# One tile's attention scores put beside the preceding tile's state and output, and the state products in two halves of the array

## The chip, the cores and the metric

The kernel runs on one core of a Trainium2 chip. TensorE (PE in the profile) multiplies matrices into PSUM, VectorE (DVE), ScalarE (ACT) and GpSimd (POOL) work on tiles, and SyncE (SP) issues most transfers. The metric is the device time of one execution in microseconds.

## The reference

A linear attention with decay, then two feed-forward parts. With B = 4, H = 8, S = 768, D = 48:

```python
for t in range(S):
    cur = np.einsum('bhd,bhe->bhde', u[None] * kt, vt)
    y[:, :, t] = np.einsum('bhd,bhde->bhe', rt, state + cur)
    state = wt[:, :, :, None] * state + np.einsum('bhd,bhe->bhde', kt, vt)
...
x = y as (3072, 384)
h = x @ w_in                                   # 384 x 2048
x = (h * clip(h + 3, 0, 6) / 6) @ w_out        # 2048 x 384
h = x @ w_in2                                  # 384 x 1024
solu = h * softmax(h); ln = layernorm(solu) * g_ln
out = ln @ w_out2                              # 1024 x 384
```

## The kernel before

**Tiles.** The sequence is cut into 6 groups of 128 steps; with 4 batches that is 24 tiles (`NTILE`), tile i being group i // 4 of batch i % 4. A tile's attention has five stages, `stw`, `st0`, `st1`, `st2`, `st3`.

`stw` clamps the decays w. `st0` brings w and r into the layout with channels on the partitions (for tiles up to 9 by transposes on TensorE, from tile 10 on, `LATE`, by VectorE's transposes in `flip`, L427) and makes running products of the decays by scans (L484, L490): q, from the end of the tile, and e, r times the inverse. `st1` brings k (kt), makes the decayed state sp and its remainder sr on GpSimd (L508, L512), q = kt times q (L518), and z = r k u. `st2` transposes q back to tokens (ktp, L532; copied to ktok by ScalarE, L534) and makes the scores pa of eight heads, the even ones on the lower, the odd ones on the upper half of the partitions (L543); GpSimd makes the masks am from the diagonal d (L550) and VectorE copies the scores into them (L554). `st3` makes the state products kv = ktok x v, two heads in one full-array product of which the diagonal blocks are used (L563), the output yt from the decayed state (L578) and from the scores (L585), four column strips of 32 at a time, the new state s_st = kv + sp (L604), and the two rounded halves of the output, xh and xl (L616, L617).

**Dense work.** The first feed-forward part goes in 96 slots (`NSLOT`), 16 for each group of four tiles: in slot n `ffn_in(n)` makes h by nine products of 512 columns (L635), ScalarE and VectorE make t, gh and gl from it (L639 to L643), and two slots later `ffn_out` uses them in nine products for y (L655). So a slot has eighteen dense products. In slots 0 to 12 the weights are still decoded (`w1_a`, `w1_b`), largely on VectorE.

**Order.** Attention stages of tiles 4 to 23 are put between `ffn_in(n)` and `ffn_out(n - 2)` by the table `sched`: tile i has `stw`, `st0`, `st1` and `st2` in the slots 4(i - 4) - 3, - 2, - 1 and 0 and `st3` in 4(i - 4) + 2. So in four slots one has the scores of a tile (`st2`), and the one two later has its output (`st3`) and the next tile's `st0`. The program order is a priority: a planner walks it with costs of its own and lets a ready instruction go ahead of one that isn't. Buffers in rotation set what can be ready: `ps_a` has three PSUM buffers that kt, wt, rt, ktp, pa, kv and yt share, `ps_h` two for h, and am has two, both of one tile. sp has one.

Of the kernel before, what the change touches and what calls it, by code (L numbers as in the profile page):

```python
# [8 lines left out]
F32 = mybir.dt.float32  # L9
# [4 lines left out]
ALU = mybir.AluOpType  # L14
# [4 lines left out]
P = 128  # L19
# [248 lines left out]
def fast_path(  # L268
# [14 lines left out]
    nc = tc.nc  # L283
    B, H, S, D = r.shape
# [5 lines left out]
    HP = H // 2  # L290
    DP = 112
# [4 lines left out]
    NTILE = NG * B  # L296
    NSLOT = NG * M1
    LAG = 2
    LATE = 10

    const = ctx.enter_context(tc.tile_pool(name="const", bufs=1, side="left"))
    dram = ctx.enter_context(tc.tile_pool(name="dram", bufs=1, space=DRAM))
# [20 lines left out]
    ps_h = left.enter_context(tc.tile_pool(name="ps_h", bufs=2, space=PSUM, side="left"))  # L323
# [6 lines left out]
        out=causal.bitcast(F32), in_=ones, pattern=[[1, P]], compare_op=ALU.is_gt, fill=0.0, base=0,  # L330
# [5 lines left out]
    atp = right.enter_context(tc.tile_pool(name="atp", bufs=2, side="right"))  # L336
# [24 lines left out]
    def w1_a(m):  # L361
        wst[m].append(dec_a(nc, dec, wst[m][0]))

    def w1_b(m):
        split(nc, dec_b(nc, *wst.pop(m)), w1_h[:, m, :], w1_l[:, m, :], nc.vector)


    s_st = []
# [5 lines left out]
    at = {}  # L374
    x_t = {}

    def load_in(i):
        g, b = divmod(i, B)
        t0 = g * C
        a = {}  # L380
        for nm, src, spare in (("w", w, "gh"), ("r", r, "gl"), ("k", k, "t")):
            if i == 2:
                t = ffp.tile([P, H, 64], F32, tag=spare, name=nm, bufs=2 if spare == "t" else 3)
            else:
                t = inp.tile([P, H, 64], F32, tag=nm, name=nm)
            nc.gpsimd.memset(t[:, :, D:64], 1.0)
            nc.sync.dma_start(out=t[:, :, 0:D], in_=src[b, :, t0:t0 + C, :].rearrange("h t d -> t h d"))
            a[nm] = t
        at[i] = a
# [34 lines left out]
    def flip(nm):  # L424

        t = ps_tile(nm + "t")
        nc.vector.transpose(  # L427
            out=t.rearrange("p h (b j) -> p h j b", j=4),
            in_=late[nm].rearrange("p h (j d) -> p h j d", d=D)[:, :, :, 0:32],
        )  # L430
        return t

    def ps_tile(nm):
        return ps_a.tile([P, 4, P], F32, tag="pa", name=nm)

    def trans(dst, src):
        s2 = src.rearrange("p h d -> p (h d)")
        for hp in range(HP):
            nc.tensor.transpose(out=dst[0:DP, hp, :], in_=s2[:, hp * P:hp * P + DP], identity=ident)

    def stw(i):
        a = at[i]
        if i >= LATE:
            x = late["w"][:, :, 0:4 * D - 16]
# [25 lines left out]
    def st0(i):  # L470
        a = at[i]
        g = i // B
        if i < LATE:
            wt = ps_tile("wt")
# [22 lines left out]
    def st1(i):  # L497
        a = at[i]
        g, b = divmod(i, B)
        q = a["q"]  # L500
        if i < LATE:
            kt = ps_tile("kt")
            trans(kt, a["k"])
        else:
            kt = flip("k")
        if g > 0:
            sp = atp.tile([P, HP, 2 * D], F32, tag="sp", name="sp", bufs=1)
            nc.gpsimd.tensor_tensor(  # L508
                out=sp[0:DP], in0=s_st[b][0:DP], in1=q[0:DP, :, 0:1].to_broadcast([DP, HP, 2 * D]), op=ALU.mult
            )  # L510
            sr = atp.tile([P, HP, 32], F32, tag="sr", name="sr", bufs=1)
            nc.gpsimd.tensor_tensor(  # L512
                out=sr[0:DP].rearrange("p h (j d) -> p h j d", j=2),
                in0=s_st[b][0:DP].rearrange("p h (j d) -> p h j d", j=2)[:, :, :, 32:D],
                in1=q[0:DP, :, 0:1].unsqueeze(3).to_broadcast([DP, HP, 2, D - 32]), op=ALU.mult,
            )
            a["sp"], a["sr"] = sp, sr
        nc.vector.tensor_tensor(out=q[0:DP, :, 1:C + 1], in0=kt[0:DP], in1=q[0:DP, :, 1:C + 1], op=ALU.mult)  # L518
        z = a["r"][:, :, 0:D]
        nc.gpsimd.tensor_tensor(out=z, in0=z, in1=a["k"][:, :, 0:D], op=ALU.mult)  # L520
        nc.gpsimd.tensor_tensor(out=z, in0=z, in1=u_bc, op=ALU.mult)
        a["z"] = z

    def st2(i):
        a = at[i]
# [30 lines left out]
    def st3(i):  # L556
        a = at[i]
        g, b = divmod(i, B)
        if g < NG - 1:
            vv = a["v"].rearrange("p h d -> p (h d)")  # L560
            kv = ps_tile("kv")
            for hp in range(HP):
                nc.tensor.matmul(  # L563
                    out=kv[0:DP, hp, 0:2 * D], lhsT=a["ktok"][:, hp, :], rhs=vv[:, hp * 2 * D:(hp + 1) * 2 * D],
                    start=True, stop=True,
                )
        y = ps_tile("yt")

        def inter(c, first):
            for q in range(4):  # L570
                if c < 2:
                    h = 4 * c + q
                    hp, f = h // 2, D * (h % 2)
                    lhs = a["sp"][0:DP, hp, f:f + 32]
                else:
                    hp = q
                    lhs = a["sr"][0:DP, q, :]
                nc.tensor.matmul(  # L578
                    out=y[32 * q:32 * q + 32, c, :], lhsT=lhs, rhs=a["e"][0:DP, hp, :], start=first, stop=not first,
                    skip_group_check=True,  # L580
                )

        def intra(c, heads, lo, n, first, last):
            for q, h in enumerate(heads):
                nc.tensor.matmul(  # L585
                    out=y[32 * q:32 * q + n, c, :], lhsT=a["v"][:, h, lo:lo + n], rhs=a["am"][h % 2][:, h // 2, :],
                    start=first, stop=last, skip_group_check=True,
                )

        for c in range(2):  # L590
            if g > 0:
                inter(c, True)
            intra(c, range(4 * c, 4 * c + 4), 0, 32, g == 0, True)
        intra(2, range(1, H, 2), 16, 32, True, False)
        intra(2, range(0, H, 2), 32, 16, True, g == 0)
        if g > 0:
            inter(2, False)
        if g < NG - 1:
            for j in range(2):
                o, f = 64 * j, D * j  # L600
                dst = s_st[b][o:o + D, :, f:f + D]
                src = kv[o:o + D, :, f:f + D]
                if g > 0:
                    nc.vector.tensor_tensor(out=dst, in0=src, in1=a["sp"][o:o + D, :, f:f + D], op=ALU.add)  # L604
                else:
                    nc.scalar.activation(out=dst, in_=src, func=ACTF.Copy)
        at.pop(i)
        if b == 0:
            x_t[g] = (
                xp.tile([P, KD, GT], F32R, tag="xh", name="xh"),  # L610
                xp.tile([P, KD, GT], F32R, tag="xl", name="xl"),
            )
        xh, xl = x_t[g]
        sl = slice(b * C, (b + 1) * C)
        xf = y[:, 0:KD, :]
        nc.scalar.activation(out=xh[:, :, sl], in_=xf, func=ACTF.Copy, accum_out=chk[:, 3 * i + 2:3 * i + 3])  # L616
        nc.vector.tensor_tensor(out=xl[:, :, sl], in0=xf, in1=xh[:, :, sl].bitcast(F32), op=ALU.subtract)  # L617
# [110 lines left out]
    def load_to(n):  # L728
        while nxt[0] < min(n, LATE):
            load_in(nxt[0])  # L730
            load_v(nxt[0])
            nxt[0] += 1
# [15 lines left out]
    NS = len(stages)  # L748
    for tick in range(starts[-1] + NS):
        for i in range(B):  # L750
            s = tick - starts[i]
# [13 lines left out]
    sched = {}  # L765
    for i in range(B, NTILE):
        for s in range(NS):
            sched.setdefault(4 * (i - B) + (s - 3 if s < NS - 1 else 2), []).append((i, s))
    for n in sorted(q for q in sched if q < 0):
        for i, s in sched[n]:  # L770
            stages[s](i)
# [2 lines left out]
    for n in range(NSLOT + LAG):  # L774
        if n < NSLOT:
            ffn_in(n)
        for i, s in sorted(sched.get(n, [])):
            stages[s](i)
            if s == 3:
                load_to(i + 3)  # L780
            if s == 2 and LATE <= i + 1 < NTILE:
                load_late(i + 1)
        if n >= LAG:
            ffn_out(n - LAG)
        if n + LD < M1:
            w1_b(n + LD)
        if n + LD + 1 < M1:
            w1_a(n + LD + 1)
        if n + LD + 3 < M1:
            w1_load(n + LD + 3)  # L790
        if n == M1:
            dec_st.close()
            late_open()
        if n == NA:
            ok = range_flag()
            right.close()
            w2_open()
            w2_load(0)
            w2_load(1)
        j = n - NA  # L800
        if 1 <= j <= 2 * M2:
            w2_b(j - 1)
        if 0 <= j < 2 * M2:
            w2_a(j)
        if 1 <= j <= 2 * M2 - 2:
            w2_load(j + 1)
# [112 lines left out]
```

## Time and profile before

| what | value |
|---|---|
| median of 3 runs | 795.32 us (794.71 to 795.42) |
| profiled execution | 796.49 us |
| its span | 794.8 us |
| mean granted clock of TensorE | 0.978 |
| TensorE busy | 753.4 us (95% of the span) |
| VectorE busy | 543.2 us (68%) |
| ScalarE busy | 331.9 us (42%) |
| GpSimd busy | 272.9 us (34%) |

The span runs from the first to the last instruction of one profiled execution. Matmuls are pipelined and overlap: the busy time of one is longer than its distance to the next, and the distance of starts tells what it takes from the queue. Instructions of one line that follow each other are drawn together in an order of time: start, length, and xcount for how many. A product in f32 is two passes, each a weight load and a matmul.

### The profile page before, as it was taken

To read this page: it belongs to the slowest core of one execution; us is meant where nothing else is said; L and a number is where in the kernel's file an instruction comes from. 1 tells how busy PE (TensorE), PEld (TensorE's weight loads), DVE (VectorE), ACT (ScalarE), POOL (GpSimd) and SP (SyncE) were. 2 spreads that over 40 slices of the span, in tenths; PEclk is the share of its full clock that TensorE was granted. 3 is DMA by queue.
4 is the path that set the end of the run, shared out by engine and by line. 5 is a ranking of instruction groups with operands and counts; after the bars stand their busy time and mean duration, and the time that the engine had idled before them with its cause. 6 is when DMAs were issued, how large, how long until landed. Compare 5 with 4: busy or idle time off the path is not lost. (4 is left out here: it accounts for less than half of the span.)

```text
span 794.8 us, 13227 instructions
## 1 busy us (share of the span) xinstructions
PE 753.4 (95%) x4922; PEld 634.3 (80%) x4922; DVE 543.2 (68%) x1038; ACT 331.9 (42%) x615; POOL 272.9 (34%) x355
## 2 busy tenths in 40 slices
PE   5689898899999999999999999999999999999996
PEld 4567676688888888888888888777889999999996
DVE  5989799856777777777777675895365555555552
ACT  3354544342334433444434334544343443443342
POOL 5487545647333333333232212231122222222210
PEclk9889799999999999999999999999999999999999
DMA  9777455235333433343323212430111111111001
GB/s 167 175 155 162 118 132 138 51 93 124 79 83 91 114 83 84 75 122 81 73 64 93 53 50 61 131 119 1 52 49 40 41 41 51 40 43 48 30 21 35
DMA packets 139432, 64.75 MB, mean 81 GB/s; under 512 B 90848, under 2 KB 133984, under 8 KB 139360
## 3 DMA queue, kind: packets, MB, share of 16 engines
q1 hardware_dynamic: 136768, 59.11, 31.2%
q10 hardware_dynamic: 2592, 4.72, 1.6%
q8 instruction: 41, 0.67, 0.4%
q14 instruction: 31, 0.25, 0.1%
HBM read 54.37 MB, written 9.44 MB: 80 GB/s over the span
## 5 line engine op out<-in xcount | busy, mean ns | idle before, releaser
L639 ACT ACTIVATE t<-h,three 128x512 f32<-128x512 f32 x96 | 65.7, 684 | 176.6 <-PE h L635 175.9
L635 PE MATMUL h<-xh,w_h 128*128 128x512 f32 x288 | 114.4, 398 | 8.7 <-DVE t L640 8.0
L655 PE MATMUL y<-gh,w_h 128*128 128x512 f32 x288 | 117.4, 408 | 0.5 <-ACT ye L661 0.5
L640 DVE SCALAR_TENSOR_TENSOR t<-t,h 128x512 f32<-128x512 f32 x96 | 65.3, 680 | 76.2 <-ACT t L639 75.9
L655 PE MATMUL y<-gl,w_h 128*128 128x512 f32 x288 | 114.0, 396 | 0.3 <-DVE gl L643 0.2
L655 PE MATMUL y<-gh,w_l 128*128 128x512 f32 x288 | 113.6, 394 | 0.0
L635 PE MATMUL h<-xl,w_h 128*128 128x512 f32 x288 | 113.5, 394 | 0.0
L635 PE MATMUL h<-xh,w_l 128*128 128x512 f32 x288 | 113.2, 393 | 0.0
L550 POOL TENSOR_TENSOR am<-ident,d 128x512 f32<-128x512 f32 x48 | 58.5, 1239 | 119.2 <-PE yt L585 119.2
L641 ACT ACTIVATE gh<-t 128x512 fp32r<-128x512 f32 x96 | 60.4, 629 | 55.0 <-DVE t L640 54.6
L643 DVE TENSOR_TENSOR gl<-t,gh 128x512 fp32r<-128x512 f32 x80 | 68.2, 853 | 20.6 <-ACT gh L641 20.4
L635 PEld LDWEIGHTS h<-xh,w_h 128*128 128x128 f32 x288 | 54.7, 190 | 22.9 <-issue 6.8
L67 DVE TENSOR_REDUCE nm<-h 128x1 f32<-128x1024 f32 x24 | 29.4, 1225 | 62.7 <-PE h L828 62.6
L655 PEld LDWEIGHTS y<-gh,w_h 128*128 128x128 f32 x288 | 54.4, 189 | 16.3 <-ACT gh L641 2.1
L855 PE MATMUL po<-w_oh,qh 128*128 128x384 f32 x192 | 67.0, 349 | 0.3 <-ACT qh L844 0.3
L855 PE MATMUL po<-w_oh,ql 128*128 128x384 f32 x192 | 65.2, 339 | 0.1
L855 PE MATMUL po<-w_ol,qh 128*128 128x384 f32 x192 | 65.0, 339 | 0.0
L655 PEld LDWEIGHTS y<-gh,w_l 128*128 128x128 f32 x288 | 54.8, 190 | 11.9
L635 PEld LDWEIGHTS h<-xl,w_h 128*128 128x128 f32 x288 | 54.8, 190 | 11.3
L635 PEld LDWEIGHTS h<-xh,w_l 128*128 128x128 f32 x288 | 54.6, 190 | 11.5
L655 PEld LDWEIGHTS y<-gl,w_h 128*128 128x128 f32 x288 | 54.7, 190 | 11.4 <-DVE gl L643 0.6
L844 ACT ACTIVATE qh<-pt 128x512 fp32r<-128x512 f32 x48 | 26.1, 595 | 79.1 <-PE pt L842 79.1
(118 smaller groups left out, 1518.6 us busy)
## 6 DMA issues: line engine op xcount, KB each, us to landing
raw<-in_moe_w_out_dram SPq DMA_DIRECT2D x24, 384.0 KB
raw<-in_moe_w_in_dram SPq DMA_DIRECT2D x48, 128.0 KB
r<-in_r_dram SPq DMA_DIRECT2D x24, 192.0 KB
k<-in_k_dram SPq DMA_DIRECT2D x24, 192.0 KB
v<-in_v_dram SPq DMA_DIRECT2D x24, 192.0 KB
y1d<-ye ACTq DMA_DIRECT2D x18, 256.0 KB
y<-y1d SPq DMA_DIRECT2D x24, 192.0 KB
out_dram<-os SPq DMA_DIRECT2D x24, 192.0 KB
```

The source lines that it names most:

```text
L67: nc.vector.tensor_reduce(out=nm, in_=h, axis=AX.X, op=ALU.max, negate=True)
L550: nc.gpsimd.tensor_tensor(out=am, in0=ident.unsqueeze(1).to_broadcast([P, HP, C]), in1=dv[:, hh, :].unsqueeze(2).to_broadcast([P, HP, C]), ...
L635: nc.tensor.matmul(out=h, lhsT=a, rhs=b, start=(j == 0), stop=(j == len(ops) - 1))
L639: nc.scalar.activation(out=t, in_=h, func=ACTF.Relu, bias=three)
L640: nc.vector.scalar_tensor_tensor(out=t, in0=t, scalar=6.0, in1=h, op0=ALU.min, op1=ALU.mult)
L641: nc.scalar.activation(out=gh, in_=t, func=ACTF.Copy)
L643: eng.tensor_tensor(out=gl, in0=t, in1=gh.bitcast(F32), op=ALU.subtract)
L655: nc.tensor.matmul(out=y_ps[g][c], lhsT=a, rhs=b, start=(m == 0 and j == 0), stop=(m == M1 - 1 and j == 2))
L844: nc.scalar.activation(out=qh[:, ms, :], in_=pt, func=ACTF.Copy)
L855: nc.tensor.matmul(out=po, lhsT=x[:, m, :], rhs=y[:, m, :], start=(n == 0), stop=(n == 3 * M2 - 1))
```

## The change

From tile 9 on (`JOIN`) the stages `stw` to `st2` come two slots earlier, and `st3` stays: `st2` of tile i + 1 and `st3` of tile i then share a slot, `st2` first, because the stages of a slot are now walked in reverse order. (That turns the order for tiles 4 to 8 too, where `st0` of tile i + 1 now stands ahead of `st3` of tile i.) The decayed state, sp and sr, leaves `st1` for a function of its own, `state_in`, which for tiles from 9 on is called behind `st3` of the tile before. kv of tiles from 8 on takes its PSUM buffer from `ps_h`. And for every tile the state products are made head by head: eight products of 48 by 48 instead of four of 112 by 96, even heads into partitions 0 to 47, odd heads into 64 to 111, so that `s_st` reads the same columns for both.

```diff
+    JOIN = 9
@@ st1
-        if g > 0:
-            sp = ...
-            sr = ...
+        if 0 < g and i < JOIN:
+            state_in(i)
@@
+    def state_in(i):
+        a = at[i]
+        b = i % B
+        q = a["q"]
+        sp = atp.tile([P, HP, 2 * D], F32, tag="sp", name="sp", bufs=1)
+        nc.gpsimd.tensor_tensor(
+            out=sp[0:DP], in0=s_st[b][0:DP], in1=q[0:DP, :, 0:1].to_broadcast([DP, HP, 2 * D]), op=ALU.mult
+        )
+        sr = ...
+        a["sp"], a["sr"] = sp, sr
@@ st3
-            vv = a["v"].rearrange("p h d -> p (h d)")
-            kv = ps_tile("kv")
-            for hp in range(HP):
+            kv = ps_tile("kv") if i < JOIN - 1 else ps_h.tile([P, HP, P], F32, tag="h", name="kv")
+            for h in range(H):
+                o = 64 * (h % 2)
                 nc.tensor.matmul(
-                    out=kv[0:DP, hp, 0:2 * D], lhsT=a["ktok"][:, hp, :], rhs=vv[:, hp * 2 * D:(hp + 1) * 2 * D],
-                    start=True, stop=True,
+                    out=kv[o:o + D, h // 2, 0:D], lhsT=a["ktok"][:, h // 2, o:o + D], rhs=a["v"][:, h, :],
+                    start=True, stop=True, skip_group_check=True,
                 )
@@
-                src = kv[o:o + D, :, f:f + D]
+                src = kv[o:o + D, :, 0:D]
@@ sched
-            sched.setdefault(4 * (i - B) + (s - 3 if s < NS - 1 else 2), []).append((i, s))
+            back = 2 if s == NS - 1 else s - 3 if i < JOIN else s - 5
+            sched.setdefault(4 * (i - B) + back, []).append((i, s))
@@ slots
-        for i, s in sorted(sched.get(n, [])):
+        for i, s in sorted(sched.get(n, []), reverse=True):
             stages[s](i)
+            if s == NS - 1 and JOIN <= i + 1 < NTILE:
+                state_in(i + 1)
```

## Rows read from the trace of the kernel before

**Rows 1.** Busy time by stretch: length, engine busy us (x count), clock, DMA share, GB/s
```profile
53.00:163.00 110.00, 94.26 (x656) 74.91 (x657) 99.23 (x160) 48.96 (x84) 68.75 (x69) 0.92 0.51 125
175.00:421.00 246.00, 246.00 (x1866) 204.47 (x1865) 177.49 (x333) 95.46 (x179) 88.47 (x103) 1.00 0.38 89
421.00:500.00 79.00, 79.00 (x571) 63.73 (x570) 55.76 (x111) 32.66 (x62) 17.10 (x19) 1.00 0.24 67
```

**Rows 2.** TensorE in order of time around the output of tile 14
```profile
300.81 0.39 PE L635 MATMUL h<-xh,w_l 128*128 128x512 f32 x1
301.04 0.93 PE L563 MATMUL kv<-v,ktok 128*112 128x96 f32 x8
301.90 0.42 PE L578 MATMUL yt<-e,sp 112*32 112x128 f32 x8
...
302.59 0.84 PE L585 MATMUL yt<-am,v 128*32 128x128 f32 x24
303.25 0.41 PE L578 MATMUL yt<-e,sr 112*32 112x128 f32 x8
303.58 0.50 PE L655 MATMUL y<-gh,w_h 128*128 128x512 f32 x1
...
321.75 0.93 PE L563 MATMUL kv<-v,ktok 128*112 128x96 f32 x8
```

**Rows 3.** TensorE in order of time around the scores of tile 15
```profile
311.89 0.55 PE L532 MATMUL ktp<-ident,q 112*128 112x112 f32 x4
312.36 1.16 PE L543 MATMUL pa<-e,q 48*128 48x128 f32 x16
313.46 0.50 PE L655 MATMUL y<-gh,w_h 128*128 128x512 f32 x1
313.79 0.39 PE L655 MATMUL y<-gl,w_h 128*128 128x512 f32 x1
```

**Rows 4.** The line of the state products: count, ns, first and last start
```profile
L563 PE MATMUL kv<-v,ktok x160: 243/262/501, 15.9 to 405.3; 128*112 128x96 f32 x160
```

**Rows 5.** TensorE in order of time, scores of tile 20, dense products behind
```profile
415.25 0.39 PE L635 MATMUL h<-xh,w_l 128*128 128x512 f32 x1
415.56 1.16 PE L543 MATMUL pa<-e,q 48*128 48x128 f32 x16
416.66 0.50 PE L655 MATMUL y<-gh,w_h 128*128 128x512 f32 x1
...
418.83 0.39 PE L635 MATMUL h<-xh,w_h 128*128 128x512 f32 x1
...
420.87 0.39 PE L655 MATMUL y<-gh,w_h 128*128 128x512 f32 x1
```

**Rows 6.** VectorE in order of time, 300 to 319 us
```profile
300.21 0.72 DVE L427 STREAM_TRANSPOSE wt<-late_w 128x512 f32<-128x512 f32 x1
302.02 0.69 DVE L640 SCALAR_TENSOR_TENSOR t<-t,h 128x512 f32<-128x512 f32 x1 [1.09 <-ACT t L639]
302.62 0.72 DVE L604 TENSOR_TENSOR s_st<-kv,sp 48x192 f32<-48x192 f32 x2
...
304.84 0.55 DVE L617 TENSOR_TENSOR xl<-yt,xh 128x384 fp32r<-128x384 f32 x1
...
310.65 0.68 DVE L518 TENSOR_TENSOR q<-kt,q 112x512 f32<-112x512 f32 x1
...
318.65 0.69 DVE L640 SCALAR_TENSOR_TENSOR t<-t,h 128x512 f32<-128x512 f32 x1 [2.68 <-ACT t L639]
```

**Rows 7.** All engines in order of time, 300 to 320 us
```profile
303.32 2.49 POOL L550 TENSOR_TENSOR am<-ident,d 128x512 f32<-128x512 f32 x2 [7.85 <-PE yt L585]
...
312.67 0.53 ACT L534 ACTIVATE ktok<-ktp 128x448 f32<-128x448 f32 x1
```

**Rows 8.** What TensorE waited for, 53 to 163 us: total, times, longest
```profile
PE h L635 <- DVE t L640: 6.9, 3, 4.6
PE rt L439 <- issue: 6.1, 4, 2.6
```

More of the change, by code (lines that the diff above doesn't have):

```diff
@@ L505, in st1 @@
             kt = flip("k")
-        if g > 0:
[L507 to L517, printed above, removed]
+        if 0 < g and i < JOIN:
+            state_in(i)
         nc.vector.tensor_tensor(out=q[0:DP, :, 1:C + 1], in0=kt[0:DP], in1=q[0:DP, :, 1:C + 1], op=ALU.mult)
@@ L522, in st1 @@
         a["z"] = z
+    def state_in(i):
[6 more added lines that the diff above has]
+        )
+        sr = atp.tile([P, HP, 32], F32, tag="sr", name="sr", bufs=1)
+        nc.gpsimd.tensor_tensor(
+            out=sr[0:DP].rearrange("p h (j d) -> p h j d", j=2),
+            in0=s_st[b][0:DP].rearrange("p h (j d) -> p h j d", j=2)[:, :, :, 32:D],
+            in1=q[0:DP, :, 0:1].unsqueeze(3).to_broadcast([DP, HP, 2, D - 32]), op=ALU.mult,
+        )
+        a["sp"], a["sr"] = sp, sr
     def st2(i):
```

## Prediction

> **What bounds the kernel now.** I read the busy time by stretch first [rows 1]. The reader is to see two regimes. From 53 to 163 us VectorE is busy for 99.23 of 110 us and TensorE for 94.26: here the first layer's weights are still decoded, and VectorE sets the pace. From 175 to 500 us TensorE is busy for the whole of both stretches at a granted clock of 1.00 (the level of 2.4 GHz), while VectorE needs 177.49 of 246 us: what leaves TensorE's queue there leaves the total. The second part of the kernel, behind 550 us, isn't touched. Next I read TensorE's instructions in order of time, around one tile's output [rows 2] and around the next tile's scores [rows 3]. From one state update to the next it is 321.75 - 301.04 = 20.71 us. Nine dense products take 420.87 - 418.83 = 2.04 us [rows 5]; a period holds eight such groups, 16.32 us. The other 4.39 us are the attention of one tile, and that is what the change rearranges, for tiles 9 to 23, nearly all in the second regime. So the question is what these 4.39 us become, and whether TensorE stays full.
>
> **The attention's 4.39 us, piece by piece.** In the scores' slot: transposes 0.47 (311.89 to 312.36) and scores 1.10 (to 313.46) [rows 3]. In the output's slot: state products 0.86 (301.04 to 301.90) and output 1.68 (to 303.58) [rows 2]. That leaves 0.28, the price of two returns to dense products, 0.14 each: the first one behind the scores is followed by the next after 0.33 us instead of 0.23 [rows 3], so 0.10 of it shows at once.
>
> **What joining removes.** With scores and output in one slot the queue goes transposes, scores, state, output, dense. One return (0.14) is gone. The state products, which followed a dense product at its own pace (300.81 to 301.04, [rows 2]) and so cost nothing to enter, now follow the scores.
>
> **What the state products cost in halves.** Now they are 8 passes for a tile (160 for 20 tiles, [rows 4]) of 112 weight columns and 96 moving columns: 0.86 us, of which 0.08 is the way out (below), 0.098 a pass. After, they are 16 passes of 48 and 48, alternately in the left and the right half of the columns. No row shows such a pass. The nearest is the output: 24 passes in four column strips, which run side by side, take 0.66 us (302.59 to 303.25), 0.0275 each, 0.11 a group of four [rows 2]. At that pace 16 passes take 0.44. To that come the first weight load, which nothing covers (0.10 for 128 columns behind the scores, so 0.04 for 48 by proportion), and the wait for the last pass before the array is used in another way (0.08: from the last h to the scores it is 415.25 to 415.56 where no transposes stand between [rows 5], 0.31 instead of 0.23). I take 0.56 us. Bound below: a pair of halves as long as 48/112 of one present pass, 0.042, eight pairs and the same ends: 0.46. Bound above: no half beside the other and every pass as long as now, 16 x 0.098 + 0.12 = 1.69. I stand near the lower end because strips and row halves do run side by side here: the 16 passes of the scores take 1.10 us, and one after another at the 0.11 of a group of the output they would take 1.76.
>
> The Trainium skill (TensorEngine Tiling (Array Packing), Key Properties) says that a change of tiling mode drains the array, and that speaks against the halves, which are a mode of their own between dense products and strips. The 0.08 us above agrees with it. By this rule tiles 4 to 7, which aren't joined, pay one drain more each.
>
> **The sum.** A joined tile with a state update: 0.47 + 1.10 + 0.56 + 1.68 + 0.14 = 3.95 against 4.39, saves 0.44 us. The last update's passes end the list at 405.3 [rows 4]; from 175 us on (405.3 - 175)/20.71 counts 12 of them: 5.3 us. Tiles 20 to 22 have none; joining saves them one entry into small products (0.08) and one return (0.14), 0.7 for the three. Total 6.0 us. With the state products at their bounds: 0.46 saves 12 x 0.54 + 0.7 = 7.2 us; 1.69 loses 12 x 0.69 - 0.7 = 7.6 us.
>
> **Edits that I cost at nothing, and their cover.** The state products of tiles 0 to 7 lie where TensorE isn't the bound; without that cover they would gain or lose some 0.3 us each. State update and decay keep their shapes; the decay moves behind the previous tile's output on GpSimd and is wanted a period later. The state products take one of the two buffers of h. So the next h waits until t has been made from the last one: done at 302.02 + 0.69, 1.9 us after the last h product began [rows 2, 6], while the next h comes only behind transposes, scores, state, output and nine y products, 6.0 us. The output's PSUM buffer is now the one that the transposes leave: ScalarE is done with it at 312.67 + 0.53 = 313.20 [rows 7], and the scores alone last until 313.46. The masks on GpSimd begin when the previous output has read its own (303.32, 2.49 us for both [rows 7]), and the scores are copied behind them: both score buffers stay taken some 4 us longer, and the next to want them are wt and rt of the tile after. No DMA is added; each load keeps its place behind st1, which moves two slots with its users, and it passes no other load on SP.
>
> **Rivals.**
>
> *VectorE late for the scores.* Now q is done at 310.65 + 0.68 = 311.33 [rows 6] and the transposes want it at 311.89, half a us later. VectorE's way from wt's flip to q is 300.21 to 311.33, 11.1 us, with the previous tile's state update and xl in it (0.72 + 0.55), 9.8 without. After, st0 and the scores are two slots with four dense groups between, 8.2 us, or 9.0 with a start 0.8 us ahead as now. That is 0.8 us late in each of 14 tiles (10 to 23): 11.2 us less 6.0, 800.5. It decides if wt's flip doesn't come 0.8 us sooner before its slot than today. Against it: VectorE has 2.68 us with nothing to do ahead of 318.65 [rows 6], and wt, rt and kt no longer queue for PSUM behind the state products and the output. 0.08, and the kernel is slower.
>
> *The halves run one after another.* 802.9 by the upper bound; against it stand strips and row halves. 0.07.
>
> *The planner doesn't join them.* Program order is only a priority in it. Where q or the output's buffer is late in its plan, dense products come between, and each break costs a return and an exit, 0.2 us: half the gain, 792.3, 0.10. That nothing at all is gained, within 0.2% (1.6 us, about what a measurement of this kernel can tell from no change): 0.07.
>
> *The first regime moves.* The reversed order puts st0(i+1) ahead of st3(i) for tiles 4 to 7. TensorE now waits 6.9 us there for t and 6.1 us for the buffer of rt [rows 8]; with wt and rt first, the output waits for a buffer instead. VectorE's work stays the same, but some 4 us to either side, part of these 13, are possible: 785.3 or 793.3, or with half a gain no change. 0.08.
>
> **How the numbers follow.** The profiled execution took 796.49 us, 1.17 above the median of 795.32 and 1.69 above its span. Less 6.0 it would be 790.5, and the median 789.3. Chances: the forecast 0.60 (its own range 787.5 to 792), half the gain 0.10, the first regime 0.08, no gain 0.07, late VectorE 0.08, halves in series 0.07. Faster is 0.60 + 0.10 + 0.04, same 0.07 + 0.02, slower 0.08 + 0.07 + 0.02. The range reaches from the gain in the first regime and the lower bound (785.5) to just past no change (796.5) and leaves out the two cases above 800.
>
> **What would show it.** In one slot of four TensorE's order is ktp x4, pa x16, kv x16, yt x56 with no dense product between; from kv to yt 0.56 us; a period of 20.27 us; TensorE full from 175 to about 495 us; q ready ahead of the transposes. Wrong: gaps or y products ahead of ktp or pa (VectorE late), over 1 us from kv to yt (halves in series), h or y between scores and output (not joined), or another start of the first h of the second group of tiles (first regime).

## The result and the profile after

The changed kernel takes 785.5 us (median of 4 runs, 785.33 to 787.12) against 795.07 us for the kernel before in the same session (4 runs, 794.71 to 795.42): a ratio of 0.9883, 95% interval 0.9867 to 0.9899. It is faster, as forecast, and 3.8 us faster than the 789.3 us that was named, on the lower edge of the range. The profiled execution took 787.12 us with a span of 785.3 us, 9.5 us less than before's span; 6.0 us were forecast. Below, spans are compared with spans.

Busy time by stretch of the changed kernel, the columns as in [rows 1]:

```profile
53.00:163.00 110.00, 97.28 (x720) 74.47 (x718) 98.46 (x163) 51.91 (x90) 75.34 (x72) 0.96 0.51 127
175.00:421.00 246.00, 246.00 (x2039) 204.17 (x2038) 175.62 (x338) 100.68 (x192) 82.85 (x104) 1.00 0.39 93
421.00:500.00 79.00, 78.36 (x512) 63.85 (x511) 58.48 (x106) 32.41 (x60) 15.98 (x18) 1.00 0.22 64
```

TensorE is as full from 175 to 421 us as it was, and VectorE needs no more there than before; in the last stretch it needs 58.48 us instead of 55.76, with TensorE at 78.36 of 79: no new bound. In the first stretch TensorE is busy for 3 us more and its granted clock rises from 0.92 to 0.96. That stretch had been costed at nothing.

TensorE in order of time around a joined slot of the changed kernel:

```profile
275.18 0.39 PE L642 MATMUL h<-xh,w_l 128*128 128x512 f32 x1
275.41 0.55 PE L539 MATMUL ktp<-ident,q 112*128 112x112 f32 x4
275.89 1.16 PE L550 MATMUL pa<-e,q 48*128 48x128 f32 x16
276.98 0.56 PE L570 MATMUL kv<-v,ktok 128*48 128x48 f32 x16
277.47 0.43 PE L585 MATMUL yt<-e,sp 112*32 112x128 f32 x8
...
278.16 0.84 PE L592 MATMUL yt<-am,v 128*32 128x128 f32 x24
278.81 0.40 PE L585 MATMUL yt<-e,sr 112*32 112x128 f32 x8
279.15 0.50 PE L662 MATMUL y<-gh,w_h 128*128 128x512 f32 x1
...
295.61 0.55 PE L539 MATMUL ktp<-ident,q 112*128 112x112 f32 x4
...
297.18 0.56 PE L570 MATMUL kv<-v,ktok 128*48 128x48 f32 x16
```

This answers to [rows 2, 3]: transposes, scores, state, output, and no dense product between them (the dots leave out output passes, and further down eight groups of dense products). The state products take 277.47 - 276.98 = 0.49 us instead of 0.86. From one update to the next it is 20.20 us, where it was 20.71.

VectorE in order of time ahead of those second transposes, which want q and e at 295.61 (compare [rows 6]):

```profile
283.22 0.72 DVE L428 STREAM_TRANSPOSE wt<-late_w 128x512 f32<-128x512 f32 x1
...
285.69 0.69 DVE L428 STREAM_TRANSPOSE kt<-late_k 128x512 f32<-128x512 f32 x1
...
289.49 0.67 DVE L509 TENSOR_TENSOR q<-kt,q 112x512 f32<-112x512 f32 x1
290.07 0.68 DVE L495 TENSOR_TENSOR e<-rt,e 112x512 f32<-112x512 f32 x1
...
298.58 0.72 DVE L611 TENSOR_TENSOR s_st<-kv,sp 48x192 f32<-48x192 f32 x2
```

Both are ready at 290.75, nearly 5 us early; before, q was 0.56 us early.

**Where the 9.5 us arise.** Slot n begins with its first h product; its start in one kernel less its start in the other shows what has been gained by then. Negative is ahead of the kernel before; "per tile" is the change over four slots between slots 41 and 61, where all joined kernels have joined tiles only. Each row is from one trace. The times come from several sessions, each with the kernel before run beside it, so that ratios compare and times less so; the kernel before alone ran from 793.1 to 798.6 us in them, and a lead of 1 or 2 us in the early columns is no more than that spread. At each of these slots TensorE has the same attention behind it in all kernels, but for joined e12: at slot 6 it has one tile's wt and rt more and half of a tile's scores less, and at slot 16 a tile's transposes and scores ahead, some 1.6 us of work.

| kernel | slot 6 | 16 | 21 | 61 | 95 | per tile | time, ratio to before |
|---|---|---|---|---|---|---|---|
| after | -5.05 | -4.25 | -2.91 | -7.91 | -9.51 | -0.50 | 785.5, 0.988 |
| e1 halves alone | -4.20 | -5.20 | -5.00 | -7.87 | -8.54 | -0.29 | 787.9, 0.990 |
| e2 joining alone | -4.79 | -2.87 | -1.03 | -1.44 | -2.22 | -0.04 | 794.3, 0.998 |
| e3 early order alone | -5.13 | -3.22 | -3.22 | -3.22 | -3.56 | 0.00 | 793.0, 0.995 |
| e4 early order undone | -1.74 | -4.83 | -0.38 | -5.38 | -7.22 | -0.49 | 788.8, 0.990 |
| e5 even heads, then odd | -5.53 | -5.00 | -3.46 | -6.56 | -7.97 | -0.31 | 788.1, 0.990 |
| e6 four strips | -5.91 | -4.00 | -2.88 | -9.71 | -11.54 | -0.68 | 784.6, 0.986 |
| e9 range checks later | -4.46 | -2.12 | -2.12 | -2.12 | -2.28 | 0.00 | 793.4, 0.997 |
| e10 joined from 13 | -3.60 | -4.17 | -3.97 | -6.98 | -8.91 | -0.50 | 786.1, 0.988 |
| e11 strips alone | 0.00 | -2.66 | -2.57 | -6.91 | -7.65 | -0.43 | 789.3, 0.992 |
| e12 strips, joined from 6 | -5.02 | 1.75 | -0.53 | -7.35 | -9.27 | -0.68 | 786.8, 0.989 |
| e13 strips, joined from 13 | 0.00 | -4.09 | -4.05 | -8.81 | -10.81 | -0.68 | 786.6, 0.989 |
| e14 e13, range checks later | -3.66 | -5.98 | -5.90 | -10.67 | -12.78 | -0.68 | 784.6, 0.986 |

At slot 21 both kernels have finished the same attention but for one joined tile (0.50), so by these two traces 2.4 us of after's gain come from the first 190 us. Then 11 tiles give 0.50 each (8.38 by slot 65), tiles 20 to 22 give 0.26 each (9.16 by slot 77), and 0.35 come in the decoding of the second part's weights, where e3 gains as much without any late edit (why is not shown).

### The profile page after: what moved, and what is told of

The parts are those of the page before. It is cut to its first block, busy times and chain, and to the rows that moved or that the text cites. A ratio compares the mean times of both kernels' runs of the same rounds, so it can differ in the third digit from the quotient of the medians.

```text
span 785.3 us, 13587 instructions
## 1 busy us (share of the span) xinstructions
PE 747.7 (95%) x5082; PEld 626.7 (80%) x5082; DVE 539.3 (69%) x1038; ACT 331.2 (42%) x615; POOL 268.5 (34%) x355
## 5 line engine op out<-in xcount | busy, mean ns | idle before, releaser
L662 PE MATMUL y<-gh,w_h 128*128 128x512 f32 x288 | 115.5, 401 | 0.6 <-ACT ye L668 0.6
L561 DVE COPY_PREDICATED am<-causal,pa 128x512 f32<-128x512 int32 x48 | 35.0, 740 | 32.8 <-POOL am L557 32.0
```

The source lines that it names most:

```text
L561: nc.vector.copy_predicated(am, causal.unsqueeze(1).to_broadcast([P, HP, C]), pa)
L662: nc.tensor.matmul(out=y_ps[g][c], lhsT=a, rhs=b, start=(m == 0 and j == 0), stop=(m == M1 - 1 and j == 2))
```

## The experiments

**The two parts one by one: e1, e2.** e1 is the kernel before with the state products in halves and nothing else; e2 is the changed kernel with full products again.

```diff
 e1 (to before)
-            for hp in range(HP):
-                nc.tensor.matmul(out=kv[0:DP, hp, 0:2 * D], lhsT=a["ktok"][:, hp, :], ...)
+            for h in range(H):
+                o = 64 * (h % 2)
+                nc.tensor.matmul(out=kv[o:o + D, h // 2, 0:D], lhsT=a["ktok"][:, h // 2, o:o + D], ...)
 e2 (to after): the same lines the other way round
```

The reads of kv in the state update follow the layout in both.

> The kernel before with the state products in halves and nothing else. Theory (the halves shorten the products, the order gives the rest): from kv to yt 0.49 us as in the changed kernel, and an entry of 0.08 between the last h and kv that the full-array products did not have, so 0.86 becomes 0.57; 12 tiles between 175 and 405 us save 0.29 each, 3.5 us in all, and the first h of slot 16 starts where it did (163.5). Rival (the 2.4 us gained before slot 21 come from the halves of tiles 4 to 7 as well): 5.9 us and slot 16 about 2 us earlier. Rival (the extra mode costs what the shorter passes give): no change.

> The changed kernel with the state products on the full array as before. Theory (order gives the first regime's gain, the joined slot one return): 0.14 for each of 12 tiles and 0.26 for each of 3, 2.5 us, and 2.4 us before slot 21, so 4.9 us below the kernel before and 4.4 above the changed one. Rival (the early gain is the halves'): 2.5 us. Rival (only halves matter, joining gives nothing): 0 to 2.4.

TensorE in order of time in e1, then in e2 (PEld is the weight loads):

```profile
314.80 0.39 PE L635 MATMUL h<-xh,w_l 128*128 128x512 f32 x1
315.12 0.57 PE L563 MATMUL kv<-v,ktok 128*48 128x48 f32 x16
315.62 0.32 PE L578 MATMUL yt<-e,sp 112*32 112x128 f32 x4
```

```profile
301.35 0.86 PEld L570 LDWEIGHTS kv<-v,ktok 128*112 128x112 f32 x8
301.36 1.02 PE L570 MATMUL kv<-v,ktok 128*112 128x96 f32 x8
302.31 0.42 PE L585 MATMUL yt<-e,sp 112*32 112x128 f32 x8
```

The weight loads of the kernel before, for the products at 301.04 of [rows 2]:

```profile
300.82 0.99 PEld L563 LDWEIGHTS kv<-v,ktok 128*112 128x112 f32 x8
```

In e1 the halves take 0.50 us (315.62 - 315.12), but the last dense product ahead of them takes 0.32 instead of the usual 0.23 [rows 2]: entering costs 0.09, and of 0.36 some 0.28 remain (0.29 a tile in the table). In e2 the full products take 0.95 instead of 0.86, so 0.09 of the 0.14 that joining saves goes back: behind scores the first full weight load starts with its product (301.35 and 301.36), where behind a dense product it starts 0.22 us ahead of it (300.82 and 301.04) and is hidden. Alone, joining gives 0.04 a tile and halves 0.29; together 0.50, since neither 0.09 is paid then: the halves' entry is gone when scores stand ahead of them, and so is the bare full weight load. The expectation of e2 (4.9 us in all) was not met: 1.4 us by medians. And e1, whose order in the program is that of before, gains 5.0 us by slot 21, as its rival had it in kind: such a gain doesn't need the joining.

**The early order: e3, e4.** e3 is the kernel before with only the stages of slots 0 to 15 in reverse order; e4 is the changed kernel with the old order there.

```diff
 e3 (to before)
-        for i, s in sorted(sched.get(n, [])):
+        for i, s in sorted(sched.get(n, []), reverse=n < 16):
 e4 (to after)
-        for i, s in sorted(sched.get(n, []), reverse=True):
+        for i, s in sorted(sched.get(n, []), reverse=n >= 16):
```

> The kernel before with the stages of a slot walked in reverse order in slots 0 to 15 alone (tiles 4 to 7: st0 of the next tile ahead of st3), not joined, full-array products. Theory (the reversed order is what gains in the first regime): 2.4 us faster, with slot 16 that much earlier. Rival (the gain is made by tile 9's stages coming two slots earlier, into a hole that TensorE has around slots 14 to 17): no change, within 0.5 us. Rival (it costs, since the output then waits for a buffer): 1 to 4 us slower.

> The changed kernel with the old order in slots 0 to 15 and the reversed one from slot 16 on. Theory (reversed order): 2.4 us slower than the changed kernel, 787.9. Rival (tile 9's earlier stages): as the changed kernel, 785.5. If both have a part, between.

e3 takes 793.0 us, ratio 0.995 [0.993, 0.997]: the order alone can give 3.2 us, all before slot 16, as its theory had it. e4, without it, is 4.8 us ahead at slot 16 as well, but loses 4.45 again until slot 21, where it is 2.5 us behind the changed kernel: TensorE waits 1.58 us there for the copies of the scores, and its granted clock is 0.79 from 168 to 176 us. So in the changed kernel the reversed order is worth about the 2.4 us that the theory of e4 named. But e1 has the old order too and keeps 5.0 us: a lead of this size doesn't need the reversed order. At slot 6 e1, e2, e3 and the changed kernel are all 4.2 to 5.1 us ahead, by four different sets of edits: what they share had to be looked for in the other engines' queues.

**A wait in ScalarE's queue: e9.** ScalarE, VectorE, TensorE and SyncE in the kernel before, 72 to 85 us:

```profile
72.99 0.37 SPq L387 DMA_DIRECT2D w<-in_w_dram  x1
...
79.45 0.61 ACT L463 ACTIVATE junk<-w,b_lo 128x384 bf16<-128x384 f32 x1 [3.53 <-DMA w<-in_w_dram]
...
80.80 0.83 ACT L60 ACTIVATE w_h<-dec 128x768 fp32r<-128x768 f32 x1
...
81.66 0.96 DVE L61 TENSOR_TENSOR w_l<-dec,w_h 128x768 fp32r<-128x768 f32 x1 [2.70 <-ACT w_h L60]
82.54 0.68 DVE L640 SCALAR_TENSOR_TENSOR t<-t,h 128x512 f32<-128x512 f32 x1
...
83.36 0.76 PE L635 MATMUL h<-xh,w_h 128*128 128x512 f32 x1 [4.57 <-DVE t L640]
```

The planner put tile 8's range checks (`junk`, wanted only at the very end) ahead of `w_h` in ScalarE's queue. The transfer of that w is issued at 72.99 and ScalarE waits 3.53 us for it; w_h, w_l, t and TensorE's h stand in a row behind. Then TensorE's clock falls, by the windows of the same kernel, to 0.50 (the level of 1.2 GHz) for the next 7.8 us:

```profile
74.00:78.00 4.00, 4.00 (x20) 3.28 (x19) 4.00 (x7) 0.85 (x1) 3.92 (x4) 1.00 1.01 229
...
83.40:91.20 7.80, 7.80 (x31) 6.18 (x32) 6.59 (x9) 3.51 (x6) 6.60 (x4) 0.50 0.32 91
```

The same engines in the changed kernel:

```profile
66.69 3.11 SPq L388 DMA_DIRECT2D w<-in_w_dram  x1
...
73.77 0.62 ACT L464 ACTIVATE junk<-w,b_lo 128x384 bf16<-128x384 f32 x1
...
78.30 0.84 ACT L60 ACTIVATE w_h<-dec 128x768 fp32r<-128x768 f32 x1
...
80.71 0.68 DVE L647 SCALAR_TENSOR_TENSOR t<-t,h 128x512 f32<-128x512 f32 x1
...
82.05 0.39 PE L642 MATMUL h<-xh,w_h 128*128 128x512 f32 x1
```

The planner has issued that load at 66.69, and ScalarE doesn't wait for it. The waits for tile 8's w in the other kernels fall in line with slot 6, roughly: none in e2, e3, e5 and e6 (4.79 to 5.91 us ahead), 0.89 us in e1 (4.20), 2.25 in e10 (3.60) and 2.12 in e4 (1.74). In e9, the kernel before, only those two range checks change places with what follows them on ScalarE (the lines that keep w_h's instruction under a name are left out here):

```diff
 e9 (to before)
+        with tc.issue_after(w_h_ins[5].ins) if i == 8 else ExitStack():
             nc.scalar.activation(out=junk, in_=a["w"][:, :, 0:D], ..., bias=b_lo, ...)
             nc.scalar.activation(out=junk, in_=a["w"][:, :, 0:D], ..., bias=b_hi, ...)
```

> The kernel before, computing the same; only tile 8's two range checks on ScalarE are queued behind the activation that makes w_h of the sixth weight block (they stood ahead of it), and no other engine's order changes. In the trace of before they wait 3.53 us for their transfer (until 79.45), and w_h, VectorE's w_l, t and h wait behind them. Theory (this queue place is what the early gain is, not the passes themselves): that wait is gone, slots 5 to 7 start 2.5 to 4 us earlier, and 2 to 3 us of it are kept at the end: 792.5 to 793.5. Rival (the lead is given back before slot 16, where VectorE waits for GpSimd): slots 5 to 7 earlier and the end within 0.5 us of before. Rival (the early gain is TensorE's shorter passes): nothing moves.

4.46 us ahead at slot 6, as much as by the edits before it; 2.1 are left at slot 16. Most of the rest is given back between slots 7 and 8, where TensorE is idle for 2.57 us ahead of rt instead of 0.64. The time is 793.4 us, ratio 0.9967 [0.9953, 0.9981], so some 2.6 us are kept. This wait is what holds the kernel before at slot 6, and whether an edit lifts it hangs on how the planner's queues happen to fall. The wait was not put back into the changed kernel, so how much of its early gain comes from here is not shown.

**What the halves are made of: e5, e6.** e5 takes the even heads first and then the odd ones, so that neighbours in the queue use the same half. e6 cuts each head's product into 32 and 16 weight columns, so that four strips are in use.

```diff
 e5 (to after)
-            for h in range(H):
+            for h in (0, 2, 4, 6, 1, 3, 5, 7):
 e6 (to after)
-                o = 64 * (h % 2)
-                nc.tensor.matmul(out=kv[o:o + D, h // 2, 0:D], lhsT=a["ktok"][:, h // 2, o:o + D], ...)
+                for lo, n in ((0, 32), (32, D - 32)):
+                    o = 64 * (h % 2) + lo
+                    nc.tensor.matmul(out=kv[o:o + n, h // 2, 0:D], lhsT=a["ktok"][:, h // 2, o:o + n], ...)
```

> The changed kernel with the state products of the four even heads first and then the four odd ones, so that successive passes use the same half. Theory (halves run side by side when they alternate): the passes follow each other at 0.045 us each, 16 x 0.045 + 0.13 = 0.85 instead of 0.49 us, 12 tiles lose 0.36 each, 4.3 us, 790. Rival (a pass is just short, alternating or not): 0.49 us and 785.5. Rival (a pass in the same half must wait out the one before it): 16 x 0.09 or more, 1.5 us and more, 12 us, 798.

> The changed kernel with each head's state product cut once more, into 32 and 16 weight columns, so that four strips run side by side as in the output and kv and yt use the array in one way: 32 passes. Theory (the change of mode costs 0.09 us and a group of four is as long as a pair): 8 x 0.045 + 0.06, from kv to yt 0.42 instead of 0.49 us, 12 tiles, 0.8 us faster than the changed kernel. Rival (32 passes with their weight loads are bound by issue, 64 instructions at 6 to 7 ns or more): 0.45 to 0.55 us, no change.

TensorE in order of time in e5, then in e6:

```profile
297.60 0.78 PE L570 MATMUL kv<-v,ktok 128*48 128x48 f32 x16
298.31 0.43 PE L585 MATMUL yt<-e,sp 112*32 112x128 f32 x8
```

```profile
296.31 0.54 PE L571 MATMUL kv<-v,ktok 128*32 128x48 f32 x32
296.67 0.40 PE L586 MATMUL yt<-e,sp 112*32 112x128 f32 x8
```

e5: 0.71 us, and 0.31 a tile instead of 0.50. The halves do run side by side, but that is worth only 0.22 us: one after another a pass costs some 0.04 (from the first start to the last it is 0.78 less the 0.21 of one pass, for 15 steps). e6: twice as many passes in 0.36 us, 0.68 a tile, 784.6 us (ratio 0.9855 [0.9837, 0.9874]); the halves were not the best cut.

**What joining costs at its start: e10, e12.** e10 joins from tile 13 on and keeps the old order until then. e12 is e6 joined from tile 6 on.

```diff
 e10 (to after)
-    JOIN = 9
+    JOIN = 13
-        for i, s in sorted(sched.get(n, []), reverse=True):
+        for i, s in sorted(sched.get(n, []), reverse=n >= 4 * (JOIN - B - 1)):
 e12 (to e6)
-    JOIN = 9
+    JOIN = 6
```

> The changed kernel with JOIN = 13, and the reversed order only from that stage on (slot 32), so that slots 0 to 31 are those of the halves alone (same queue orders there). Theory (the halves alone reach slot 21 5.0 us ahead of before, the changed kernel only 2.9, since bringing tile 9 two slots forward costs 2 us around slots 16 to 20): 5.3 us ahead at slot 23, then 0.29 for tiles 9 to 11, 0.49 for 12 to 19 and 0.26 for 20 to 22, about 11 us at the end: 784. Rival (two slots are lost wherever the stages are brought forward): 786.

> The kernel after with strips, and the joining from tile 6 on instead of 9, so that the one-time entry lies at slots 4 to 7, where weights are still decoded and VectorE sets the pace. Theory (the entry costs the 1.3 to 4 us because two tiles' vector work falls into one tile's time just where TensorE becomes the bound, slots 15 to 20): with the entry moved forward TensorE is 4 to 5 us ahead of before at slot 21 instead of 2.9, and the span 12.5 to 14 us below before's. Rival (the vector work pulled forward delays the decoding by as much wherever it is put): 2 to 3.5 us ahead at slot 21 and the span 11 to 12 us below, as with tile 9. The later tiles' period, 20.05 us, is the same in both.

In e10 the first h of slot 32 is 4.83 us ahead of before and that of slot 37 only 3.98, with one tile's 0.50 gained in between: the start of joining costs 1.3 us once, and the rival of e10 came out. After pays 1.8 between slots 16 and 21 (4.25 to 2.91 ahead, and one tile's 0.50), of which 0.5 may be no cost of joining, since e1 loses as much there (5.20 to 5.00 ahead, and one tile's 0.29). TensorE in order of time in e10 shows how:

```profile
245.57 0.55 PE L539 MATMUL ktp<-ident,q 112*128 112x112 f32 x4
245.88 0.48 PE L662 MATMUL y<-gh,w_h 128*128 128x512 f32 x1
...
246.76 1.16 PE L550 MATMUL pa<-e,q 48*128 48x128 f32 x8
247.84 0.50 PE L662 MATMUL y<-gh,w_h 128*128 128x512 f32 x1
...
249.66 1.16 PE L550 MATMUL pa<-e,q 48*128 48x128 f32 x8
```

Two tiles' vector work falls into one tile's time there (VectorE is busy for 9.85 of the 10 us from 244 to 254), and the scores are cut in two with dense products between, presumably because the planner expects VectorE late; half of the scores takes 1.08 us (246.76 to 247.84), as long as all of them, so that the cut costs about what the start does. e12 was to hide that where VectorE sets the pace anyway, and the theory behind it fell: it is ahead by only 0.53 us at slot 21, where e6 is by 2.88; 786.8 us. TensorE's waits in e12 in order of time point to a reason:

```profile
112.63 0.77 PE L643 MATMUL h<-xh,w_h 128*128 128x512 f32 x1 [2.36 <-DVE t L648]
126.31 0.86 PE L571 MATMUL kv<-v,ktok 128*32 128x48 f32 x32 [3.29 <-DVE t L648]
```

Now the state products wait for t: their buffer is one of h's two, and it comes free only when VectorE has made t. What costs nothing where TensorE is the bound costs 3.29 us once, and 4.8 us in three waits, where VectorE is. That this is all of e12's loss is not shown.

**Parts put together: e11, e13, e14.** e11 is e1 with e6's strips; e13 is e10 with them; e14 is e13 with e9's edit, and that changes the places of four ScalarE instructions and of nothing else on any engine.

> The kernel before with one part alone: the state products head by head, and each head's product cut into 32 and 16 weight columns (four strips of the array); no joining, old order, kv in its old buffer pool. Theory (the strips' saving is a shorter run of passes and doesn't depend on what stands in front of it): between the state products and the output 0.36 us instead of 0.49 in halves, period 20.43 - 0.17 = 20.26 us; the early stretch goes as in the run with halves alone, since all queue orders should be the same (4.0 to 5.2 us ahead of before at slot 21); span 10 to 11 us below before's, so some 0.5 to 1.5 us longer than joined strips. Rival (leaving a dense product for strips costs more than leaving scores for strips, because scores are row strips already): h to kv 0.3 or more instead of 0.32, period 20.35 or more, span only 9 us below before's.

> The joining from tile 13 on with the old order before it (as in the earlier run with that edit), and the state products in four strips for all tiles. Theory (gains of strips and of a later joining add up): 8.91 + 11 x 0.165 = 10.7 us below before's span; the early stretch like that of strips alone. Rival (the early stretch is chance within 1 to 2 us between runs): anything from 9.5 to 12.5 us, with the difference all ahead of slot 21.

> The previous kernel (four strips, joining from tile 13) with one more edit, the one tried before on its own: ScalarE takes tile 8's two range checks behind w_h and t of the weight block that follows, instead of waiting for the transfer of that tile's w in front of them. Four ScalarE instructions change places and nothing else does on any engine. Theory (the wait of 3.2 us in ScalarE's queue at 76 to 79 us is what that kernel lost again at slots 4 to 6): slot 6 some 4 us ahead of before (was 0.0), slot 21 5 to 6 us ahead (was 4.05), span 1 to 2 us below that kernel's 783.9, so the fastest of the study. Rival (what is won there is eaten up again by VectorE's work at slots 8 to 14, as three quarters of it were in the earlier run with this edit alone): slot 6 4 us ahead, but slot 21 within 0.5 us of 4.05 and the span 783.4 to 784.4.

By the tile all three do what was expected: 0.43 without joining, 0.68 with it. The early stretch was expected wrongly for e11 and e13, and with it the span of e11 (7.4 us below before's instead of 10 to 11): the strips changed the planner's queues once more, and ScalarE again waits 3.73 and 3.18 us for the same load (0.00 us ahead at slot 6 in both). That makes e14 a second trial of the cause. ScalarE, VectorE and TensorE in e14:

```profile
77.34 0.85 ACT L60 ACTIVATE w_h<-dec 128x768 fp32r<-128x768 f32 x1 [1.97 <-DVE dec L53]
...
78.98 0.61 ACT L467 ACTIVATE junk<-w,b_lo 128x384 bf16<-128x384 f32 x1 [0.23 <-DMA w<-in_w_dram]
...
80.24 0.47 PE L646 MATMUL h<-xh,w_h 128*128 128x512 f32 x1 [2.25 <-DVE t L651]
```

w_h is 3 us earlier, slot 6 is 3.66 us ahead instead of 0.00, and by the traces half of it stays: 782.0 us of span against 783.9, medians 784.57 and 786.64. That half is not clear of noise: the two ran in different sessions, the intervals of their ratios overlap ([0.9834, 0.9875] and [0.9865, 0.9906]), and e11 and e13, which have equal queues there, differ by 1.5 us at slot 21. e14 and e6 are the fastest kernels of the study and can't be told apart (ratios 0.9855 [0.9834, 0.9875] and [0.9837, 0.9874]).

## Why the prediction came out as it did

**The sum for a joined tile was right, and small in one term.** 0.44 us were forecast and 0.50 measured. The term is the state products in halves: 0.56 forecast, 0.49 found, 0.03 above the lower bound. The way there is confirmed in its parts. The 0.14 of a return and the bare weight load, 0.10 for 128 columns, show in e2, which takes 0.09 us longer over its full products and so saves 0.04. The rule of the Trainium skill (TensorEngine Tiling (Array Packing), Key Properties), that a change of tiling mode drains the array, was read as one drain more where dense products stand ahead of the halves; e1 agrees, with 0.09 us at each entry. Tiles 20 to 22 gave 0.26 each for 0.22.

**Where it failed: "Edits that I cost at nothing".** The step said that the state products of tiles 0 to 7 lie where TensorE isn't the bound, and let the first regime count for nothing. Of the 3.5 us by which the span's gain was underestimated, 2.4 lie there, 0.7 in the joined tiles and 0.35 in the second part's decoding. TensorE's waits of the changed kernel, against [rows 8]:

```profile
PE y L662 <- POOL gl L650: 2.7, 1, 2.7
PE h L642 <- ACT w_h L60: 2.4, 2, 1.2
PE h L642 <- DVE t L647: 2.3, 2, 1.9
```

The wait for t of 4.6 us is gone, and so are the 6.1 us ahead of rt, for which the profile shows no releaser and which the prediction read as a wait for a buffer. The rival "the first regime moves" named the stretch, these two waits and the size, 4 us, with 0.08, and put it down to the reversed order; it was taken as a case of its own, where it came on top of the forecast. Behind the wait for t the rival saw no cause. e9 and e14 show one: a load's place on SyncE and a wait behind it in ScalarE's queue. The time ahead of rt is down to 0 to 1.6 us in the kernels with the reversed order in slots 0 to 15 (after, e2, e3, e5, e6), and e4 speaks for that order; but e1 gains as much with that time still there:

```profile
PE rt L439 <- issue: 6.2, 4, 2.4
```

So how the 2.4 us divide between the order and the queues stays open. The sentence "it passes no other load on SP" was written of program order; the planner's queues moved even in e1, which changes nothing but the state products: SyncE issues this w there ahead of a load of v that it follows in the kernel before.

**How near it came, and luck.** The forecast's own range, 787.5 to 792 us, is missed by 2 us. The whole range holds the result on its very edge, because its lower end was set by the rival of the first regime (785.3) and the lower bound of the halves, and here both came to pass in part: the early stretch gave 2.4 us of the 4, and the halves took 0.49 us, near their bound of 0.46. That the result lies inside is in part luck.

**The rivals.** VectorE isn't late: q is done 5 us ahead, because the way from wt's flip to q shrank from 11.1 to 6.9 us (283.22 to 290.16): of what stood in it, the wait of 1.09 us, the state update and xl [rows 6] have left, and the rival had taken out the last two alone; one of two t's has left too, and e comes behind q instead of ahead of it. The halves don't run one after another, and even if they did (e5), the kernel would be faster: the upper bound had every pass as long as a present one, 0.098, and it takes 0.04. The planner does join the tiles throughout, but not at the start; that one-time cost of 1.3 to 1.8 us was in no term. Halves alone (e1) end at 786.5 us of span, the changed kernel at 785.3: of the 0.21 a tile and 0.26 for tiles 20 to 22 that joining adds, 3.3 us in all, some 1 us is left by these traces. The start of joining takes 1.3 to 1.8 of the rest, and the remainder lies within early differences that no edit explains.

**What stays open.** Of the early gains the wait at 79 us is shown. A second one, between slots 14 and 16, is not: e1 gains 2.5 us there and e9 nothing. It is not VectorE's wait for z of tile 8, which is as long in e1 as in the kernel before (before, then e1):

```profile
159.88 0.55 DVE L539 TENSOR_REDUCE d<-r 128x8 f32<-128x384 f32 x1 [3.10 <-POOL r L521]
```

```profile
157.06 0.55 DVE L539 TENSOR_REDUCE d<-r 128x8 f32<-128x384 f32 x1 [3.47 <-POOL r L521]
```

VectorE's and GpSimd's orders differ around it in the two kernels, and none of that was tried by itself. Nor do the early gains repeat closely: e11 and e13 have the same queues on all engines until they are joined, and are 2.57 and 4.05 us ahead at slot 21; e1 and e10, a pair of the same kind, 5.00 and 3.97. Differences of 1.5 us there are not explained by any edit.

## What to carry to other kernels

Before a change is costed at nothing in a stretch, look which instruction there waits for a transfer while others stand behind it on its engine: where a planner orders the queues, an edit elsewhere can lift such a wait (e2, e3) or bring it back (e11, e13), and here it was worth 3.7 to 4.5 us where it stood (e14, e9) and some 2.6 us in the end (e9), about a quarter of what the whole change brought. When two edits meet in one place, run each alone: halves gave 0.29 us a tile, joining 0.04, both 0.50. And work that nobody waits for belongs behind what others wait for: the four ScalarE instructions moved in e9 are the cheapest 2 us of this study.

## What the runs showed of the hardware

- Sixteen state passes of 48 by 48 take 0.71 us in one half after the other, 0.49 alternately; the same work in 32 passes over four strips takes 0.36, ends included: more and smaller passes were faster.
- From dense products into two halves the next start comes after 0.32 us instead of 0.23 (e1). A full weight load of 112 columns behind the scores starts with its product instead of 0.22 us ahead of it, and the eight full passes take 0.95 us instead of 0.86 (e2).
- Half of the scores (8 passes into one PSUM buffer, so one half of the rows by the code) takes 1.08 us in e10, all 16 take 1.09 in the changed kernel (275.89 to 276.98): the second half of the rows cost nothing.
- After 4.57 us without work TensorE ran at a granted clock of 0.50 for 7.8 us, and in e14 at 0.56 for 7.7 us after a wait of 2.25 us: a wait was paid for a second time.
